# Two more m quarters used unsplit, state reads grouped by pairs, and a wider issue gate in a float32 attention and FFN kernel

## The chip, the cores and the metric

The kernel runs on one core of one Trainium2 chip, in one launch. The metric is the device time of that launch in microseconds; lower is better. "PE" is the matmul engine (TensorE), "PEld" its weight loads, "DVE" the vector engine, "ACT" the scalar engine, "POOL" GpSimd and "SP" the engine that issues the transfers.

## The reference

```python
scores = scale * np.matmul(x, state.transpose(0, 1, 3, 2))   # x: 8 x 8 x 512 x 64, state: 8 x 8 x 32 x 64
scores = scores - scores.max(-1, keepdims=True)
a = np.exp(scores)
a /= a.sum(-1, keepdims=True) + 1e-09
xread = np.matmul(a, state)
scores2 = scale * np.matmul(state, x.transpose(0, 1, 3, 2))
...
sread = np.matmul(a2, x)
attn = np.concatenate([xread, sread], axis=2)
...
h = x @ w_in          # x: 4608 tokens x 512, w_in: 512 x 2048
g = h - np.tanh(h)
return g @ w_out      # w_out: 2048 x 512
```

Everything is float32. `a2` is the softmax of `scores2` over the 512 positions. The 4608 tokens are the 8 x 512 positions read from the state (`xread`) and the 8 x 32 state rows (`sread`).

## The kernel before

**What is multiplied.** `xread` is never formed. For each batch `b` the state is multiplied with `w_in` first: `m` (256 rows of heads and state slots, 2048 columns, held in four quarters `q` of 512 columns), and then `h = a @ m`. The hidden part of a chunk (`Chunk(i)`, one batch `b` of 512 tokens, or the 256 rows of `sread` as the last chunk) has 16 blocks `f` of 128 columns; for each block PE writes one PSUM bank `hps`, ACT takes `tanh` of it into `t`, DVE subtracts (`t = hps - t`), and the output part multiplies `g` with the rows `f` of `w_out` (`wo`) into four banks `ops`, one per 128 tokens, that gather over all `f`.

**Split operands.** A float32 operand is split into two fp32r parts, `hi` and `lo`, by `split`: ACT casts (line 97), DVE subtracts (line 98). A product is then three fp32r matmuls (lines 397 to 399 for the hidden part, 437 to 439 for the output). This holds for `m`, for the attention weights `at` (their split form is `aT`), for `g` and for `wo`. Only quarter 0 of chunk 0 is used unsplit: there `m_first[0]` and the unsplit weights `ats` go into plain float32 matmuls (lines 599 and 395), which the profile shows as two records each.

**The start.** `w_in` and `w_out` come as 64-bit numbers and are made float32 on the chip (`Weight.steps`: three DVE passes, lines 127, 128 and 131, one ACT pass, line 130). The first part is written out by hand as the string `SEQ`; its op `D` is a matmul on a blank tile into a bank that nobody reads, `S` the scores of batch 0, `c`, `T`, `M`, `B`, `E`, `Z`, `N`, `A` the softmax chain of batch 0 up to the transposed weights `ats`. Right behind it `split_first` splits these weights. `m_first_two` multiplies the state of batches 0 and 1 with a row block of `w_in` (line 164) and copies the two halves of the bank to `m_first[q]` and `m_second[q]`.

**The order afterwards.** A list of 144 steps `(chunk, f)`: blocks 0 to 7 of chunk 0, all of chunk 1, blocks 8 to 15 of chunk 0, then chunks 2 to 8. In step `st` the hidden part of step `st + 2` and the output part of step `st` are written. Side work (attention of later batches, conversion of weights, `m` of later batches) is cut into units by `yield`, and tables (`SCH`, `D0`) say at which step each unit is written; `tc.issue_after(x)` keeps what is written inside it behind instruction `x` in the scheduler's order. For steps below `GATED` all side work stands behind the tanh and the subtraction of its step. A scheduler then fixes one order for each engine; each engine runs its queue in that order.

**State reads.** `state_read(b, ss)` is the `sread` part: for each half `hf` (four heads) an exponential of the scores, four PE transposes into `pps`, an ACT copy to `pt`, 16 matmuls of 32 x 64 with the positions `xn` into `rps` (line 351), and four small DVE multiplications into `sr`.

Of the kernel before, what the change touches and what calls it, by code (L numbers as in the profile page):

```python
# [26 lines left out]
EPS = 1e-9  # L27
LAG = 2
HALF = 8
GATED = 48  # L30
EARLY_S = 2
# [4 lines left out]
def attention_ffn(ctx: ExitStack, tc: tile.TileContext, xT, xn, bd, bh, sp, sm, sl, win, wout, xout, sout):  # L36
# [209 lines left out]
    def attention(b, aT):  # L246
# [51 lines left out]
        for hf in range(2):  # L298
            e = es[hf]
            ef = e.rearrange("p a n -> p (a n)")  # L300
            z = pool.tile([P, 16, 1], F32, tag="z", name=f"z{b}{hf}")
            nc.vector.reduce_sum(z, e, axis=AX.X)
            nc.vector.tensor_scalar_add(z, z, EPS)
            nc.vector.reciprocal(z, z)
            nc.vector.tensor_mul(e, e, z.broadcast_to([P, 16, 32]))
            at = pool.tile([P, 512], F32, tag="at", name=f"at{b}{hf}", bufs=1)
            nc.vector.transpose(at, ef)
            yield split(aT[:, 0, hf], aT[:, 1, hf], at)
        if b >= EARLY_S:
# [9 lines left out]
    def split_first():  # L319
        for hf in range(2):  # L320
            split(aTs[0][:, 0, hf], aTs[0][:, 1, hf], ats[hf])

    def state_read(b, ss):
        for hf in range(2):

# [16 lines left out]
            pt = pool.tile([P, 4, P], F32, tag="p2t", name=f"p2t{b}{hf}", bufs=PTB)  # L342
            nc.scalar.copy(pt, ps)
            yield

            w = 1
            ps = bank(ps_a, f"rps{b}{hf}")[:, : 64 * w]
            for k in range(4):
                for c in range(4 // w):
                    cs = slice(32 * w * c, 32 * w * c + 32 * w)  # L350
                    nc.tensor.matmul(  # L351
                        ps[cs], pt[:, k, cs], xr[:, k, 64 * w * c : 64 * w * c + 64 * w], start=(k == 0), stop=(k == 3)
                    )
            for j in range(4):
                h = 4 * hf + j
                js = slice(32 * j, 32 * j + 32)
                nc.vector.tensor_scalar_mul(
                    sr[b // 4][32 * (b % 4) : 32 * (b % 4) + 32, 64 * h : 64 * h + 64],
                    ps[js, 64 * (j % w) : 64 * (j % w) + 64],
                    ri[js],  # L360
                )
            yield

# [11 lines left out]
    class Chunk:  # L375
# [5 lines left out]

        def prepare(self, q):
            self.m[q] = load_m(self.i, q) if self.i < B else load_win(q)

        def hidden(self, f):

            i, n = self.i, self.n
            ps = bank(ps_h, f"hps{i}_{f}")[:, :n]
            cols = slice((f % 4) * P, (f % 4) * P + P)
            mhi, mlo = self.m[f // 4]  # L390
            ahi, alo = aTs[i][:, 0], aTs[i][:, 1]
            nk = 2 if i < B else 4
            for k in range(nk):
                if mlo is None:
                    nc.tensor.matmul(ps, mhi[k][:, cols], ats[k], start=(k == 0), stop=(k == 1))
                    continue
                nc.tensor.matmul(ps, mhi[k][:, cols], ahi[:, k], start=(k == 0), stop=False)  # L397
                nc.tensor.matmul(ps, mhi[k][:, cols], alo[:, k], start=False, stop=False)  # L398
                nc.tensor.matmul(ps, mlo[k][:, cols], ahi[:, k], start=False, stop=(k == nk - 1))  # L399
            self.finish(f, ps)  # L400
# [143 lines left out]
    def step(op):  # L544
# [133 lines left out]
    for st, (i, f) in enumerate(steps):  # L678
# [87 lines left out]
```

## Time and profile before

| | |
|---|---|
| three timed runs | 676.95, 679.95, 681.13 us (median 679.95) |
| the profiled execution | 677.02 us, of which the span of the instructions is 675.2 us |
| PE busy | 653.2 us, 97% of the span |
| DVE busy | 462.1 us, 68% |
| ACT busy | 376.5 us, 56% |
| HBM traffic | 146 GB/s over the span |
| mean granted clock of PE | 0.996 of full speed |

The shares are means over the whole span, and the first tenth of it is unlike the rest: the page's row of forty slices shows DVE at 9 tenths in slices 2, 5 and 6 and PE below that in the first two, and from slice 6 on PE at 9 tenths in every slice to the end, with DVE down to 4 to 7. A matmul's record in the trace is longer than the time until the next one may start, so the starts of neighbouring matmuls are the measure of what one costs.

### The profile page before, as it was taken

What the parts mean: (1) busy time and instruction counts of PE and PEld (TensorE: products, weight loads), DVE (VectorE), ACT (ScalarE), POOL (GpSimd) and SP (SyncE); (2) the same over time, 40 slices, a digit from 0 to 9 for tenths busy, and PEclk for the clock granted to TensorE, in tenths of its full rate; (3) what the DMA queues carried; (4) which work ended last, traced back from release to release, by engine and by line L of the source; (5) the groups of instructions that cost most, each with busy time, mean ns of one, the idle gap of its engine ahead of it and who ended that gap; (6) DMA issues with size and microseconds to landing.
All of it is one profiled execution on the core that took longest, in us unless ns stands there. A gap on an engine that the chain in (4) does not pass through costs nothing.

```text
span 675.2 us, 9423 instructions
## 1 busy us (share of the span) xinstructions
PE 653.2 (97%) x3456; PEld 516.2 (76%) x3456; DVE 462.1 (68%) x811; ACT 376.5 (56%) x667; POOL 1.2 (0%) x7
## 2 busy tenths in 40 slices
PE   5699899999999999999999999999999999999997
PEld 2356677887888877787888787887778788888996
DVE  5989898969766469857975497647664686444442
ACT  3696487867755556855656365535443454333442
POOL 0000000000000000000000000000000000000000
PEclk9899999999999999999999999999999999999999
DMA  8586386566565642825345344553251212000300
GB/s 301 167 289 270 143 274 215 171 186 212 175 193 183 164 167 103 260 83 183 111 164 164 94 128 161 177 168 138 95 172 63 94 63 94 1 29 26 135 31 32
DMA packets 45935, 99.25 MB, mean 147 GB/s; under 512 B 6081, under 2 KB 11457, under 8 KB 45889
## 3 DMA queue, kind: packets, MB, share of 16 engines
q1 hardware_dynamic: 45888, 98.65, 45.0%
q8 instruction: 27, 0.44, 0.3%
q14 instruction: 20, 0.16, 0.1%
HBM read 66.65 MB, written 31.98 MB: 146 GB/s over the span
## 4 chain that ended last, share of the span: by engine, by line
PE 85%; DVE 8%; ACT 2%; DMA 2%; issue 1%; SPq 0%; ACTq 0%; DVEq 0%
PE ops L437 17%; PE ops L439 16%; PE ops L438 16%; PE hps L397 9%; PE hps L398 9%; PE hps L399 9%; PE mps L200 2%; PE rps L351 1%; PE sps L275 1%; PE pps L341 1%; PE mps L164 1%; DMA mr<-md 1%; PE mps L199 1%; DVE m L98 1%; DMA xT<-in_xT 1%
## 5 line engine op out<-in xcount | busy, mean ns | idle before, releaser
L437 PE MATMUL ops<-wo,g 128*128 128x512 f32 x544 | 214.1, 398 | 1.5 <-ACT wo L97 1.5
L438 PE MATMUL ops<-wo,g 128*128 128x512 f32 x544 | 213.0, 392 | 0.0
L439 PE MATMUL ops<-wo,g 128*128 128x512 f32 x544 | 199.2, 391 | 0.3 <-DVE g L98 0.3
L405 DVE TENSOR_TENSOR t<-hps,t 128x512 f32<-128x512 f32 (+1 forms) x142 | 93.5, 658 | 94.5 <-ACT t L405 93.8
L405 ACT ACTIVATE t<-hps 128x512 f32<-128x512 f32 (+1 forms) x142 | 81.3, 573 | 130.1 <-PE hps L399 127.1
L437 PEld LDWEIGHTS ops<-wo,g 128*128 128x128 f32 x544 | 102.6, 189 | 29.8 <-ACT wo L97 3.7
L97 ACT CAST g<-t 128x512 fp32r<-128x512 f32 (+1 forms) x142 | 84.4, 596 | 66.5 <-DVE t L405 63.1
L98 DVE TENSOR_TENSOR g<-t,g 128x512 fp32r<-128x512 f32 (+1 forms) x142 | 93.3, 659 | 41.0 <-ACT g L97 39.3
L439 PEld LDWEIGHTS ops<-wo,g 128*128 128x128 f32 x544 | 102.0, 188 | 23.7 <-issue 1.6
L438 PEld LDWEIGHTS ops<-wo,g 128*128 128x128 f32 x544 | 102.2, 188 | 21.4 <-issue 1.0
L397 PE MATMUL hps<-aT,m 128*128 128x512 f32 x248 | 98.8, 400 | 2.5 <-ACT aT L97 1.4
L398 PE MATMUL hps<-aT,m 128*128 128x512 f32 x248 | 97.1, 392 | 0.2 <-DVE aT L98 0.2
L399 PE MATMUL hps<-aT,m 128*128 128x512 f32 x248 | 96.9, 391 | 0.0
L397 PEld LDWEIGHTS hps<-aT,m 128*128 128x128 f32 x248 | 46.4, 188 | 16.4 <-ACT aT L97 2.7
L399 PEld LDWEIGHTS hps<-aT,m 128*128 128x128 f32 x248 | 46.6, 188 | 11.4 <-DVE wor L127 0.8
L398 PEld LDWEIGHTS hps<-aT,m 128*128 128x128 f32 x248 | 46.6, 188 | 10.7 <-DVE aT L98 1.1
L98 DVE TENSOR_TENSOR wst<-w,wst 64x512 fp32r<-64x512 f32 x64 | 43.9, 686 | 14.7 <-ACT wst L97 12.9
L201 ACT COPY st<-mps 128x512 f32<-128x512 f32 x64 | 36.5, 587 | 18.2 <-PE mps L200 18.1
L98 DVE TENSOR_TENSOR m<-mr,m 128x1024 fp32r<-128x1024 f32 x31 | 37.8, 1220 | 11.2 <-ACT m L97 10.8
L97 ACT CAST wst<-w 64x512 fp32r<-64x512 f32 x64 | 39.6, 619 | 0.8
L97 ACT CAST m<-mr 128x1024 fp32r<-128x1024 f32 x31 | 32.3, 1045 | 7.1 <-DMA mr<-md 7.0
L200 PE MATMUL mps<-wst,sms 128*128 128x512 f32 x64 | 24.9, 395 | 0.0
(216 smaller groups left out, 577.5 us busy)
## 6 DMA issues: line engine op xcount, KB each, us to landing
md<-st SPq DMA_DIRECT2D x128, 128.0 KB, 2.3
mr<-md SPq DMA_DIRECT2D x26, 512.0 KB, 3.8
xT<-in_xT SPq DMA_DIRECT2D x16, 512.0 KB, 4.8
w<-wf SPq DMA_DIRECT2D x16, 512.0 KB, 4.3
xn<-in_xn SPq DMA_DIRECT2D x16, 512.0 KB, 3.4
out_x<-ob SPq DMA_DIRECT2D x32, 256.0 KB, 2.4
wn<-wf SPq DMA_DIRECT2D x8, 512.0 KB, 4.1
ml<-md SPq DMA_DIRECT2D x8, 512.0 KB, 3.8
```

The lines of the kernel that those rows point to most:

```text
L97: nc.scalar.copy(hi, src)
L98: return (sub or nc.vector).tensor_sub(lo, src, hi)
L164: nc.tensor.matmul(ps, sps[:, p], wfs[q, k][:, c], start=True, stop=True)
L200: nc.tensor.matmul(ps, s[:, 0, h], t[:, e], start=(g == 1), stop=True)
L201: nc.scalar.copy(stage[:, e], ps)
L397: nc.tensor.matmul(ps, mhi[k][:, cols], ahi[:, k], start=(k == 0), stop=False)
L398: nc.tensor.matmul(ps, mhi[k][:, cols], alo[:, k], start=False, stop=False)
L399: nc.tensor.matmul(ps, mlo[k][:, cols], ahi[:, k], start=False, stop=(k == nk - 1))
L405: tanhs.append((nc.scalar.activation(t, ps, AF.Tanh).ins, nc.vector.tensor_sub(t, ps, t).ins))
L437: nc.tensor.matmul(o, g[:, 0, tok], wo[:, f, 0], start=first, stop=False)
L438: nc.tensor.matmul(o, g[:, 0, tok], wo[:, f, 1], start=False, stop=False)
L439: return nc.tensor.matmul(o, g[:, 1, tok], wo[:, f, 0], start=False, stop=last).ins
```

## The change

- Quarter 1 of chunk 0 and quarter 0 of chunk 1 are used unsplit, as quarter 0 of chunk 0 was: 8 blocks `f` with two float32 matmuls in place of six fp32r ones, and no split of these two quarters of `m`.
- The weights `aT` of batch 0 are split in steps 9 and 10 in place of right after `SEQ`. Those of batch 1 are kept unsplit in a tile `both` (tag `x`) and split in step 9, as units of their own. `ats` of batch 0 gets buffers of its own.
- Six more `D` at the head of `SEQ`.
- `state_read` does the transposes of both halves first, then the 32 matmuls of both into one bank, then the eight multiplications. Its number of units stays four.
- `GATED` goes from 48 to 144.
- Tables: `a0` [58, 60, 62, 64] becomes [58, 58, 59, 59], `r1` [74, 76, 78, 80] becomes [74, 74, 75, 75], `att0` [2, 3, 4, 5, 5, 6] becomes [2, 3, 4, 5, 5, 9, 9, 10].

```diff
+UNSPLIT = {0: 2, 1: 1}
...
-GATED = 48
+GATED = 144
...
-            at = pool.tile([P, 512], F32, tag="at", name=f"at{b}{hf}", bufs=1)
+            if b == 1:
+                if hf == 0:
+                    both = pool.tile([P, 2, 512], F32, tag="x", name="at1", bufs=XB)
+                at = both[:, hf]
+            else:
+                at = pool.tile([P, 512], F32, tag="at", name=f"at{b}{hf}", bufs=1)
             nc.vector.transpose(at, ef)
-            yield split(aT[:, 0, hf], aT[:, 1, hf], at)
+            if b == 1:
+                ats[1][hf] = at
+            if b != 1:
+                split(aT[:, 0, hf], aT[:, 1, hf], at)
+            yield
+        if b == 1:
+            for hf in range(2):
+                yield split(aT[:, 0, hf], aT[:, 1, hf], both[:, hf])
...
     def split_first():
         for hf in range(2):
-            split(aTs[0][:, 0, hf], aTs[0][:, 1, hf], ats[hf])
+            yield split(aTs[0][:, 0, hf], aTs[0][:, 1, hf], ats[0][hf])
...
             nc.scalar.copy(pt, ps)
+            pts.append(pt)
+            xrs.append(xr)
+            ris.append(ri)
             yield
-            w = 1
-            ps = bank(ps_a, f"rps{b}{hf}")[:, : 64 * w]
+        ps = bank(ps_a, f"rps{b}").rearrange("p (g n) -> p g n", g=2)[:, :, :64]
+        for hf in range(2):
             for k in range(4):
-                for c in range(4 // w):
-                    cs = slice(32 * w * c, 32 * w * c + 32 * w)
+                for c in range(4):
+                    cs = slice(32 * c, 32 * c + 32)
                     nc.tensor.matmul(
-                        ps[cs], pt[:, k, cs], xr[:, k, 64 * w * c : 64 * w * c + 64 * w], start=(k == 0), stop=(k == 3)
+                        ps[cs, hf], pts[hf][:, k, cs], xrs[hf][:, k, 64 * c : 64 * c + 64], start=(k == 0), stop=(k == 3)
                     )
+        yield
...
         def prepare(self, q):
+            if q < UNSPLIT.get(self.i, 0):
+                r = (m_first, m_second)[self.i][q]
+                self.m[q] = [r[:, k] for k in range(2)], None
+                return
...
-                    nc.tensor.matmul(ps, mhi[k][:, cols], ats[k], start=(k == 0), stop=(k == 1))
+                    nc.tensor.matmul(ps, mhi[k][:, cols], ats[i][k], start=(k == 0), stop=(k == 1))
...
             advance(a0, D0["a0"].count(st))
+            if st in [9, 10]:
+                next(first_split)
```

What the scheduler made of it, first on PE, at the output of block 1 of chunk 0 (`ops` from `g_1`), with the product of state and `w_in` for quarter 1 (`mps`) around it. Before:

```order
L437 MATMUL ops_0_3_354<-wo,g_1_266 128x512
L164 MATMUL mps_347<-w_320,sps 128x512
L438 MATMUL ops_0_0_351<-wo,g_1_266 128x512
L439 MATMUL ops_0_0_351<-wo,g_1_266 128x512
L438 MATMUL ops_0_1_352<-wo,g_1_266 128x512
```

And now:

```order
L459 MATMUL ops_0_3_356<-wo,g_1_272 128x512
L417 MATMUL hps_4_422<-at_209,mr_304 128x512
L417 MATMUL hps_5_460<-at_209,mr_304 128x512
L165 MATMUL mps_349<-w_322,sps 128x512
L460 MATMUL ops_0_0_353<-wo,g_1_272 128x512
```

The first float32 halves of blocks 4 and 5 of chunk 0 now stand there; their second halves stand within the output of block 3. Before, all of blocks 4 and 5 stood behind the output of block 3.

On DVE, from the subtraction `t_0` of chunk 1 on (`w` and `wor` are conversions of `w_in` and `w_out`). Before:

```order
L405 TENSOR_TENSOR t_0_624<-hps_0_617,t_0_624 128x512
L127 TENSOR_SCALAR w_679<-w20d 128x512
L127 TENSOR_SCALAR w_679<-w21d 128x512
L127 TENSOR_SCALAR wor_695<-wo8d 128x512
L128 SCALAR_TENSOR_TENSOR w_679<-w20d,w_679 128x512
L128 SCALAR_TENSOR_TENSOR w_679<-w21d,w_679 128x512
L405 TENSOR_TENSOR t_1_649<-hps_1_642,t_1_649 128x512
L127 TENSOR_SCALAR w_734<-w22d 128x512
L128 SCALAR_TENSOR_TENSOR wor_695<-wo8d,wor_695 128x512
L98 TENSOR_TENSOR g_0_627<-t_0_624,g_0_627 128x512
```

And now, from the subtraction `t_1` on:

```order
L427 TENSOR_TENSOR t_1_616<-hps_1_613,t_1_616 128x512
L128 TENSOR_SCALAR w_697<-w22d 128x512
L129 SCALAR_TENSOR_TENSOR wor_662<-wo8d,wor_662 128x512
L99 TENSOR_TENSOR aT_124<-at_209,aT_124 128x512
L132 ISA w_646<-w_646,w20r 128x1024
L99 TENSOR_TENSOR aT_431<-at_562,aT_431 128x512
L132 ISA w_646<-w_646,w21r 128x1024
L99 TENSOR_TENSOR aT_431<-at_562,aT_431 128x512
L99 TENSOR_TENSOR g_0_598<-t_0_595,g_0_598 128x512
```

The rows from `t_0` to `t_1` are as before; between `t_1` and the `lo` part of `g_0` three of the four moved splits and two conversion passes have come in.

On PE, at the state read of batch 2, with the hidden block 2 of chunk 2 around it. Before, the first half (`pps` are the transposes of the second):

```order
L399 MATMUL hps_2_1911<-aT_1283,m_1783 128x512
L397 MATMUL hps_2_1911<-aT_1283,m_1783 128x512
L351 MATMUL rps_1687<-xn_1590,p2t_1597 32x64 x16
L341 MATMUL pps_1719<-ident,s_1401 128x128 x4
L398 MATMUL hps_2_1911<-aT_1283,m_1783 128x512
```

And now, where both halves stand, one block later:

```order
L461 MATMUL ops_0_1_1891<-wo,g_0_1775 128x512
L420 MATMUL hps_3_1906<-aT_1250,m_1762 128x512
L369 MATMUL rps_1672<-xn_1557,p2t_1564 32x64 x16
L369 MATMUL rps_1672<-xn_1663,p2t_1670 32x64 x16
L200 MATMUL mps_1711<-wst_1705,sms_1051 128x512
```

Two stretches of 16 became one of 32. In the whole order there were 16 such stretches, and there are 9: seven of 32 and two of 16.

## Rows read from the trace of the kernel before

**Rows 1.** Windows: stretch, its length; PE, PEld, DVE, ACT, POOL busy us; clock; DMA share; GB/s.
```profile
77.00:115.00 38.00, 37.66 (x150) 28.21 (x151) 35.47 (x64) 29.45 (x52) 0.00 (x0) 1.00 0.67 235
115.00:660.00 545.00, 544.73 (x3012) 441.11 (x3011) 358.61 (x627) 295.94 (x522) 0.00 (x0) 1.00 0.41 131
```

**Rows 2.** Timeline, start and length in us: neighbouring fp32r matmuls, float32 weight loads.
```profile
34.29 0.39 PE L438 MATMUL ops<-wo,g 128*128 128x512 f32 x1
34.52 0.39 PE L439 MATMUL ops<-wo,g 128*128 128x512 f32 x1
...
35.63 0.19 PEld L395 LDWEIGHTS hps<-at,mr 128*128 128x128 f32 x1 [0.24 <-issue]
36.06 0.19 PEld L395 LDWEIGHTS hps<-at,mr 128*128 128x128 f32 x1 [0.24 <-issue]
```

**Rows 3.** Timeline, PE, hidden blocks 0 to 2 of chunk 1.
```profile
72.07 0.73 PE L397 MATMUL hps<-aT,m 128*128 128x512 f32 x2 [1.00 <-ACT aT L97]
...
77.34 0.50 PE L397 MATMUL hps<-aT,m 128*128 128x512 f32 x1 [1.02 <-DVE t L405]
```

**Rows 4.** Timeline of the start, POOL and DVE.
```profile
0.87 0.53 POOL L530 MEMSET blank<- 128x512 f32 x1
...
18.62 0.69 DVE L98 TENSOR_TENSOR aT<-at,aT 128x512 fp32r<-128x512 f32 x1
19.23 0.25 DVE L569 RECIPROCAL z<-z 128x16 f32<-128x16 f32 x1
```

**Rows 5.** Timeline, PE, 39 to 53 us; in brackets idle time before and its end.
```profile
39.77 1.20 PE L437 MATMUL ops<-wo,g 128*128 128x512 f32 x4 [0.98 <-ACT wo L97]
...
45.05 1.19 PE L437 MATMUL ops<-wo,g 128*128 128x512 f32 x4 [0.50 <-ACT wo L97]
...
50.62 0.39 PE L397 MATMUL hps<-aT,m 128*128 128x512 f32 x1
...
52.54 1.06 PE L275 MATMUL sps<-xT,bdr 64*32 64x512 f32 x8 [0.85 <-DMA xT<-in_xT]
```

**Rows 6.** Tile xT: scores matmuls, length in ns (least, median, most).
```profile
L275 PE MATMUL sps<-xT,bdr x112: 587/589/614, 52.5 to 532.5; 64*32 64x512 f32 x112
...
L551 PE MATMUL sps<-xT,bdr x8: 1057/1074/1116, 6.6 to 9.3; 128*64 128x512 f32 x8
```

**Rows 7.** Timeline, DVE, 49 to 80 us.
```profile
49.01 1.22 DVE L98 TENSOR_TENSOR m<-mr,m 128x1024 fp32r<-128x1024 f32 x1
50.14 0.69 DVE L128 SCALAR_TENSOR_TENSOR wor<-wo5d,wor 128x512 uint32<-128x512 uint32 x1
...
71.12 1.25 DVE L460 COPY ob<-ops 128x512 f32<-128x512 f32 x2
72.30 0.67 DVE L98 TENSOR_TENSOR aT<-at,aT 128x512 fp32r<-128x512 f32 x1
73.00 0.71 DVE L307 STREAM_TRANSPOSE at<-e 128x512 f32<-128x512 f32 x1
...
76.59 0.69 DVE L405 TENSOR_TENSOR t<-hps,t 128x512 f32<-128x512 f32 x1 [1.50 <-ACT t L405]
...
79.41 0.69 DVE L405 TENSOR_TENSOR t<-hps,t 128x512 f32<-128x512 f32 x1
```

**Rows 8.** Timeline, PE, around 16 state-read matmuls (32 records) of a half.
```profile
488.56 0.39 PE L398 MATMUL hps<-aT,m 128*128 128x512 f32 x1
488.88 0.65 PE L351 MATMUL rps<-xn,p2t 128*32 128x64 f32 x32
...
489.80 0.40 PE L439 MATMUL ops<-wo,g 128*128 128x512 f32 x1
```

**Rows 9.** Timeline, PE, around the eight scores matmuls (16 records) of batch 2.
```profile
151.99 0.39 PE L438 MATMUL ops<-wo,g 128*128 128x512 f32 x1
152.31 1.09 PE L275 MATMUL sps<-xT,bdr 64*32 64x512 f32 x16
...
153.67 0.39 PE L437 MATMUL ops<-wo,g 128*128 128x512 f32 x1
```

More of the change, by code (lines that the diff above doesn't have):

```diff
@@ L320, in split_first @@
         for hf in range(2):
-            split(aTs[0][:, 0, hf], aTs[0][:, 1, hf], ats[hf])
+            yield split(aTs[0][:, 0, hf], aTs[0][:, 1, hf], ats[0][hf])
     def state_read(b, ss):
+        pts, xrs, ris = [], [], []
         for hf in range(2):
@@ L343, in state_read @@
             nc.scalar.copy(pt, ps)
+            pts.append(pt)
+            xrs.append(xr)
+            ris.append(ri)
             yield
-            w = 1
-            ps = bank(ps_a, f"rps{b}{hf}")[:, : 64 * w]
+        ps = bank(ps_a, f"rps{b}").rearrange("p (g n) -> p g n", g=2)[:, :, :64]
+        for hf in range(2):
             for k in range(4):
-                for c in range(4 // w):
-                    cs = slice(32 * w * c, 32 * w * c + 32 * w)
+                for c in range(4):
+                    cs = slice(32 * c, 32 * c + 32)
                     nc.tensor.matmul(
-                        ps[cs], pt[:, k, cs], xr[:, k, 64 * w * c : 64 * w * c + 64 * w], start=(k == 0), stop=(k == 3)
+                        ps[cs, hf], pts[hf][:, k, cs], xrs[hf][:, k, 64 * c : 64 * c + 64], start=(k == 0), stop=(k == 3)
                     )
+        yield
+        for hf in range(2):
             for j in range(4):
@@ L357, in state_read @@
                 nc.vector.tensor_scalar_mul(
-                    sr[b // 4][32 * (b % 4) : 32 * (b % 4) + 32, 64 * h : 64 * h + 64],
-                    ps[js, 64 * (j % w) : 64 * (j % w) + 64],
-                    ri[js],
+                    sr[b // 4][32 * (b % 4) : 32 * (b % 4) + 32, 64 * h : 64 * h + 64], ps[js, hf], ris[hf][js]
                 )
-            yield
+        yield
     def turn_sread():
@@ L466, in attention_ffn @@
     aTs = [None] * (B + 1)
-    ats = [None] * 2
+    ats = [[None] * 2 for _ in range(2)]
     def new_attention(b):
@@ L572, in step @@
         elif k == "A":
-            ats[j] = pool.tile([P, 512], F32, tag="ob", name=f"at0{j}", bufs=OB)
-            o(nc.vector.transpose(ats[j], es[j]))
+            ats[0][j] = pool.tile([P, 512], F32, tag=f"at0{j}", name=f"at0{j}", bufs=1)
+            o(nc.vector.transpose(ats[0][j], es[j]))
         elif k in "abrp":
@@ L598, in step @@
             i = "hH".index(k)
-            o(nc.tensor.matmul(hps[j], m_first[0][:, i, j * P : j * P + P], ats[i], start=(i == 0), stop=(i == 1)))
+            o(nc.tensor.matmul(hps[j], m_first[0][:, i, j * P : j * P + P], ats[0][i], start=(i == 0), stop=(i == 1)))
         elif k == "X":
@@ L624, in attention_ffn @@
     RE = json.loads('[1, 0, 0, 1]')
-    SEQ = 'a0 r0 b0 p0 S0 c0 T0 S1 D D M0 c1 B0 T1 E0 D D M1 B1 a1 r1 E1 b1 m0 k0 p1 Z0 N0 D A0 m1 k1 Z1 N1 D A1 a2 r2 h0 H0 h1 H1 b2 X0 p2 G0 X1 m2 a3 r3 b3 p3 D m3 k2 D G1 k3'
+    SEQ = 'D D D D D D a0 r0 b0 p0 S0 c0 T0 S1 D D M0 c1 B0 T1 E0 D D M1 B1 a1 r1 E1 b1 m0 k0 p1 Z0 N0 D A0 m1 k1 Z1 N1 D A1 a2 r2 h0 H0 h1 H1 b2 X0 p2 G0 X1 m2 a3 r3 b3 p3 D m3 k2 D G1 k3'
     for op in SEQ.split():
@@ L633, in attention_ffn @@
     a0 = state_read(0, ss)
-    split_first()
+    first_split = split_first()
     late1 = late_read(1)
@@ L647, in attention_ffn @@
     atts = {}
-    SCH = dict(json.loads('{"conv": [0, 1, 8, 8, 9, 10, 11, 12, 13, 14], "pair": [0, 1, 9, 9, 10, 11, 12, 13, 14, 15], "a0": [58, 60, 62, 64], "att0": [2, 3, 4, 5, 5, 6], "att1": [21, 22, 23, 24, 25, 26, 28, 28, 30], "att2": [5, 9, 9, 13, 13, 13, 13, 13, 13], "m0": [17, 18, 19, 20, 21, 22, 23, 24, 25, 26, 27, 28, 30, 31, 33, 35], "m1": [40, 46, 52, 53, 53, 54, 55, 57, 62, 62, 62, 65, 73, 77, 79, 84], "wo": [0, 1, 2, 3, 4, 5, 6, 8, 10, 12, 13, 15, 17, 18, 19], "r1": [74, 76, 78, 80]}'))
+    SCH = dict(json.loads('{"conv": [0, 1, 8, 8, 9, 10, 11, 12, 13, 14], "pair": [0, 1, 9, 9, 10, 11, 12, 13, 14, 15], "a0": [58, 58, 59, 59], "att0": [2, 3, 4, 5, 5, 9, 9, 10], "att1": [21, 22, 23, 24, 25, 26, 28, 28, 30], "att2": [5, 9, 9, 13, 13, 13, 13, 13, 13], "m0": [17, 18, 19, 20, 21, 22, 23, 24, 25, 26, 27, 28, 30, 31, 33, 35], "m1": [40, 46, 52, 53, 53, 54, 55, 57, 62, 62, 62, 65, 73, 77, 79, 84], "wo": [0, 1, 2, 3, 4, 5, 6, 8, 10, 12, 13, 15, 17, 18, 19], "r1": [74, 74, 75, 75]}'))
     D0 = dict(
```

## The prediction

> **What bounds the kernel now.** The page's busy shares come first, PE at 97%, but a record of a PE that waits inside a run counts as busy too, so the share alone cannot say whether there is anything to win. The windows say where: from 115 to 660 us PE is busy for 544.73 of 545 us, with DVE at 359 and ACT at 296 [rows 1]. The starts of neighbouring matmuls show that this is real work: an fp32r matmul of 512 columns starts every 0.23 us (34.29, 34.52), and I use 0.227, which repeats through the steady part [rows 2]. From the last long wait on (77.34 us, block 2 of chunk 1 waiting for the bank of block 0) PE's queue never stands still for half a microsecond [rows 1, 3]. So the time is the moment at which PE becomes continuously fed, now 77 us, plus the PE work left after it. Only two things can help: reach that moment sooner, or take work off PE. Before that moment DVE is the engine behind which the others wait: its queue of conversions and softmax steps runs almost without a gap, and PE waits at 39.77 and 45.05 us for a converted weight, at 72.07 us for the split of the weights of batch 1, and at 77.34 us for a subtraction [rows 3, 5].
>
> **The blank matmuls and the start.** PE stands idle until 6.6 us, so the six blanks cost nothing if they end by then: six times two records of 256 columns. The scores of batch 0 are eight records of 512 columns, issued as four pairs that start between 6.6 and 9.3 us, 0.9 us from pair to pair [rows 6]; half of that is 0.45, and twelve come to 5.4 us from 1.4 us on, when the blank tile is written [rows 4]: 6.8 at that slow pace, sooner at a better one, and the first scores' data is there at 6.6. So between 0 and 0.2 us lost. What they may give: the scores take 1074 ns a record, a like float32 form later 589 ns [rows 6], as if the first ones ran at the lower of the two clock levels (1.2 GHz, not 2.4), although the clock row has no lower entry there. With the upper level, the first scores and so the DVE chain behind them come up to 0.9 us earlier; with the lower one, none. I take 0.5 of the -0.2 to 0.9. *The Trainium skill (TensorE: Matmul & The Clock Gate, Part 1) says that half clock is the default and activity releases it, which would give the full 0.9; no run here shows whether these blanks are enough. By it the sum below would be 0.4 us better.*
>
> **Splits taken out of the DVE chain.** The first split of batch 0's weights stands between two steps of the softmax chain (18.62, next at 19.23): 0.6 us [rows 4]. The second falls where DVE waits for a tanh anyway: 0. So all that follows the start moves by s = 0.6 + 0.5 = 1.1 us (0.5 to 1.5), and ACT, which has no gap of its own work in the stretch behind, passes it on. In the stretch of 49 to 74 us DVE loses two splits of m (1.13 us of queue each: 49.01 to 50.14), the first split of batch 1's weights (0.7: 72.30 to 73.00) and the two copies of finished outputs that stood ahead of the last transpose (1.18: 71.12 to 72.30) [rows 7]: 4.1 us. The last transpose, which ended at 73.7, then ends at 69.6 - s.
>
> **Unsplit blocks on PE.** A float32 record starts 0.43 us after the one before it (35.63, 36.06), a float32 matmul of 512 columns is two of them, 0.86 us [rows 2]. A block costs 2 x 0.86 = 1.72 us in place of 6 x 0.227 = 1.36: PE gets 0.36 more for each of eight blocks. It pays where PE waits anyway. I follow PE's queue in the new order, in the times of before less s:
> - Until the end of block 3's output (50.62 us before [rows 5]) the float32 halves of blocks 4 and 5 come in, 4 x 0.86 = 3.44. They fill the wait of 0.50 at 45.05 and some 0.15 more: 53.4.
> - Then the scores of batch 1 in one run instead of two, 1.2 us (its price is worked out below; their input lands at about 52.5 [rows 5], which is in time), blocks 6 and 7 (3.44) and 48 output matmuls (10.9): 69.0. Before, PE came to this place at 71 and waited.
> - Blocks 0 and 1 of chunk 1 need no split: their first halves need the first transpose, their second halves (70.7) the last one (69.6). PE does not wait; it ends at 72.4. Block 2 needs the bank of block 0: tanh and subtraction after 71.6. Before, the subtraction began at 76.59 and block 2 at 77.34 [rows 7, 3]; with a tanh of 0.6 it starts at 73.2 where it was 77.34. That is 4.1 us, and s on top.
> - Given back: blocks 2 and 3 cost 0.36 more each (0.7). Block 3 needs the bank of block 1, and five conversion passes are queued on DVE ahead of that subtraction, which came 2.8 us behind the first (76.59, 79.41 [rows 7]): from 72.6 on it ends at 76.1. PE, which now comes at 74.9, waits some 1.1 us.
>
> Front: 4.1 + 1.1 - 0.7 - 1.1 = 3.4 us won.
>
> **The moved splits.** All four of the weights' splits now come to DVE right after that, at 0.6 us each, 2.4 us, in a stretch where DVE is busy for 35.47 of 38 us [rows 1]. What hides them: DVE starts this stretch 4 us earlier too, and PE waited for nothing in it. Behind the three that stand ahead of `g_0`'s low part waits only the last third of block 0's output, which PE's queue reaches two float32 matmuls and eight output matmuls later. I take 0; if the cover is gone, up to the whole front gain.
>
> **State reads in one group.** A run of 16 state-read matmuls takes PE from 488.56 to 489.80 us, 1.24 us, of which two ordinary matmuls are 0.45: 0.79 us. The 32 records themselves follow each other at 14 ns (0.45); the other 0.34 us is the change to another shape and back [rows 8]. Seven runs fewer save 7 x 0.34 = 2.4 us; I take 2.0, since before some runs shared that change with transposes next to them. *The Trainium skill (TensorEngine Tiling (Array Packing), Key Properties) says that changing the tiling mode drains the engine, which the row agrees with. (TensorE: Matmul & The Clock Gate, Part 3, the mechanism) adds only about 4 ns for each further tile; the row shows 14 ns a record. By the page's price a group of 32 would cost 0.3 us less and the sum would be 2.3 us better; the row's price stands in the sum.* The scores of one later batch stand in one run less: a run costs 153.67 - 151.99 - 0.45 = 1.2 us [rows 9], nearly all of it the same change of shape. Together 3.2 us less PE work after the front.
>
> **The gate.** In the stretch that it adds, PE has 0.27 us of idle time in 545 [rows 1]; there is nothing to win. It could cost, if weights of a next batch came late: from 0 up to the rival below. I take 0.
>
> **Sum.** 3.4 + 1.2 + 2.0 = 6.6 us. The profiled execution of before took 677.02 us (675.2 us of span), which gives 670.4; against the median of the three runs, 679.95, it is 673.4, and I give that, as medians are what will be compared. The runs of before lie 4 us apart, so a change below 1% (6.8 us) can hardly be told from none.
>
> **The rivals.**
> 1. *The front gain is given back.* PE becomes fed 3.4 us sooner, but DVE has no less to do before 115 us apart from two m splits (2.3 us), and if a conversion (weights of block 8, m of quarter 2) is the next thing late, PE waits there. For it: DVE at 93% in that window [rows 1]. Against it: not one wait of PE there before. Then 3.2 us stay: 676.7.
> 2. *More than the sum.* The blanks give 0.9, DVE is less loaded than I count and the 1.1 us at block 3 does not come: 6.6 + 0.4 + 1.1 = 8.1: 671.9.
> 3. *Slower: the grouped state read stops PE's queue.* The queue is strict, and all that follows a group waits with it. Before, the first half's matmuls needed one copy and one load; a group needs both. In the new order the group stands some 20 ordinary matmuls, 4.5 us, behind the second half's transposes. If exponential, transposes, copy and load of `xn` take longer than that on queues that now carry side work behind every tanh, each of eight reads stops PE for the rest. It decides from 0.8 us a read on (8 x 0.8 = 6.6); for over 1% slower it takes 1.7. With 2.5 us: 8 x 2.5 - 6.6 = +13.4, 693. Against it: the same copies and loads were never waited for in 545 us.
> 4. *The change does not do what it says.* Had the scheduler left its order as it was, the time would stay at 679.95; the order shows the moves, so this has no chance of its own.
>
> **How the numbers follow.** The forecast (gains of 4 to 7.5 us) 0.54, rival 1 0.20, rival 2 0.20, rival 3 0.06. Faster by over 1% needs more than 6.8 us: all of rival 2 and a third of the forecast, 0.38. Slower by over 1% is rival 3, 0.06. Within 1%: 0.56. The range takes in rival 1 (676.7) and rival 2 (671.9), with 2 us on each side for the spread of the runs: 670 to 678.5.
>
> **What would show it.** Right: float32 records of blocks 4 and 5 between 38 and 52 us, block 2 of chunk 1 starting near 72 us, four splits on DVE near 76 to 82 us, PE idle in 115 to 660 us still under 1 us, 32-matmul state reads of about 1.24 us. Wrong: PE waiting between 75 and 110 us for a DVE conversion (rival 1), or before state reads (rival 3); scores of batch 0 still at 1074 ns a record (no clock gain).

## The result and the profile after

| | median | runs | ratio to before, 95% interval |
|---|---|---|---|
| before, beside the first runs | 679.87 us | 676.95 to 681.13, 6 | |
| changed kernel | 670.11 us | 668.49 to 671.66, 6 | 0.9879 [0.9855, 0.9902] |
| changed kernel once more, other chip | 669.56 us | 667.80 to 670.31, 6 | 0.9859 [0.9830, 0.9888] |

Faster, by 1.2 to 1.4%, 8 to 10 us by the ratios. The profiled execution of the changed kernel took 671.66 us, that of before 677.02: only 5.4 us apart. Why two profiles lie 5.4 us apart and two medians 9.8 is half of what the experiments were for.

Windows of the changed kernel (stretch, its length; PE, PEld, DVE, ACT, POOL busy; clock; DMA share; GB/s), against [rows 1]:
```profile
77.00:115.00 38.00, 37.68 (x147) 27.61 (x148) 35.90 (x64) 29.59 (x52) 0.00 (x0) 1.00 0.74 249
115.00:660.00 545.00, 545.00 (x3044) 445.94 (x3043) 358.76 (x630) 297.23 (x525) 0.00 (x0) 1.00 0.41 131
```
PE still has no idle time behind 115 us, and the time is still "when PE becomes continuously fed, plus the work left". So I read each run by two numbers: the start of block 2 of chunk 1 (77.34 us before [rows 3]), and the rest, the span minus it. Before: 675.2 - 77.3 = 597.9 us.

Timeline, PE, hidden blocks 0 to 3 of chunk 1 in the changed kernel's first profile:
```profile
70.30 3.59 PE L417 MATMUL hps<-at,mr 128*128 128x512 f32 x8
74.51 1.98 PE L417 MATMUL hps<-at,mr 128*128 128x512 f32 x4 [0.61 <-DVE t L427]
77.32 1.13 PE L417 MATMUL hps<-at,mr 128*128 128x512 f32 x2 [0.83 <-DVE t L427]
```
The same in its second profile (run f1_after_again):
```profile
68.14 3.59 PE L417 MATMUL hps<-at,mr 128*128 128x512 f32 x8
72.35 1.98 PE L417 MATMUL hps<-at,mr 128*128 128x512 f32 x4 [0.61 <-DVE t L427]
75.16 1.12 PE L417 MATMUL hps<-at,mr 128*128 128x512 f32 x2 [0.83 <-DVE t L427]
```
Equal patterns, 2.2 us apart; the rest is 595.4 in both. Most of what moved the first one is in the windows of these two executions around 40 us:
```profile
40.31:43.72 3.41, 3.41 (x5) 1.51 (x5) 3.41 (x8) 2.67 (x5) 0.00 (x0) 0.50 1.00 306
```
```profile
40.00:43.40 3.40, 3.40 (x10) 1.83 (x11) 3.40 (x8) 2.95 (x5) 0.00 (x0) 1.00 0.86 276
```
In the first profile the granted clock was at the lower level (0.50, 1.2 GHz) from 40.3 to 43.7 us, and PE got half as many records done; in the second at the upper one (2.4 GHz). Timeline, PE, the matmuls ahead of and behind that stretch, in the first profile and then in the second:
```profile
39.34 1.28 PE L459 MATMUL ops<-wo,g 128*128 128x512 f32 x4 [2.03 <-ACT wo L98]
...
43.91 1.02 PE L165 MATMUL mps<-w,sps 128*128 128x512 f32 x2
```
```profile
38.75 1.19 PE L459 MATMUL ops<-wo,g 128*128 128x512 f32 x4 [0.98 <-ACT wo L98]
...
41.75 1.02 PE L165 MATMUL mps<-w,sps 128*128 128x512 f32 x2
```
The first profile ran 0.6 us late ahead of the fall (39.34, 38.75) and 2.2 late after it (43.91, 41.75), so this fall cost 1.6 us. The 0.6 was there before; the first profile had another fall at 19.8 us, the second one at 27.5.

Tile xT, the scores of batch 0 (length in ns: least, median, most), in the changed kernel and then without its six blanks (run e1_no_blanks); before it was 1074 [rows 6]:
```profile
L573 PE MATMUL sps<-xT,bdr x8: 592/618/643, 6.6 to 8.6; 128*64 128x512 f32 x8
```
```profile
L573 PE MATMUL sps<-xT,bdr x8: 1061/1061/1114, 6.5 to 9.2; 128*64 128x512 f32 x8
```
Timeline, DVE, of the changed kernel's first profile, against [rows 7]: the last transposes right ahead of the copies, and the four splits of attention weights behind the two subtractions (the first and the last are shown):
```profile
69.27 1.30 DVE L314 STREAM_TRANSPOSE at<-e 128x512 f32<-128x512 f32 x2
70.49 1.25 DVE L482 COPY ob<-ops 128x512 f32<-128x512 f32 x2
73.76 0.69 DVE L427 TENSOR_TENSOR t<-hps,t 128x512 f32<-128x512 f32 x1 [2.02 <-ACT t L427]
...
76.60 0.67 DVE L427 TENSOR_TENSOR t<-hps,t 128x512 f32<-128x512 f32 x1
...
78.13 0.67 DVE L99 TENSOR_TENSOR aT<-at,aT 128x512 fp32r<-128x512 f32 x1
...
83.28 0.67 DVE L99 TENSOR_TENSOR aT<-at,aT 128x512 fp32r<-128x512 f32 x1
```
Timeline, PE, a grouped state read, against [rows 8]:
```profile
481.98 0.39 PE L421 MATMUL hps<-aT,m 128*128 128x512 f32 x1
482.30 1.10 PE L369 MATMUL rps<-xn,p2t 128*32 128x64 f32 x64
483.33 0.50 PE L419 MATMUL hps<-aT,m 128*128 128x512 f32 x1
483.67 0.40 PE L420 MATMUL hps<-aT,m 128*128 128x512 f32 x1
```
From 481.98 to 483.67, less two ordinary matmuls (0.45): 1.23 us for 64 records, against 0.79 for 32. So 32 more records cost 0.45, 14 ns each, and the change of shape is 0.34 us, as worked out. The Trainium skill (TensorE: Matmul & The Clock Gate, Part 3, the mechanism) has some 4 ns for a further tile of a pack. Here only four column strips take turns, each many times, and a record adds 14 ns, so the page's price is not one for these groups.

### The profile page after: what moved, and what is told of

Same layout as the page of the kernel before. It is cut to its first block, busy times and chain, and to the rows that moved or that the text cites. A ratio compares the mean times of both kernels' runs of the same rounds, so it can differ in the third digit from the quotient of the medians.

```text
span 669.9 us, 9418 instructions
## 1 busy us (share of the span) xinstructions
PE 654.2 (98%) x3452; PEld 517.9 (77%) x3452; DVE 458.7 (68%) x809; ACT 375.0 (56%) x665; POOL 1.2 (0%) x7
## 3 DMA queue, kind: packets, MB, share of 16 engines
q1 hardware_dynamic: 45888, 98.65, 45.4%
## 4 chain that ended last, share of the span: by engine, by line
PE 95%; DVE 2%; ACT 1%; DMA 1%; issue 0%; POOL 0%; ACTq 0%; DVEq 0%; POOLq 0%
PE ops L459 19%; PE ops L460 18%; PE ops L461 18%; PE hps L419 9%; PE hps L420 9%; PE hps L421 9%; PE mps L201 2%; PE hps L417 2%; PE sps L276 1%; PE mps L165 1%; PE rps L369 1%; PE mps L200 1%; PE pps L356 1%; DMA wo2d<-in_wout 1%; PE warm L569 1%; PE hps L621 1%
## 5 line engine op out<-in xcount | busy, mean ns | idle before, releaser
L419 PE MATMUL hps<-aT,m 128*128 128x512 f32 x232 | 91.6, 395 | 0.0
L420 PE MATMUL hps<-aT,m 128*128 128x512 f32 x232 | 90.8, 391 | 0.0
L421 PE MATMUL hps<-aT,m 128*128 128x512 f32 x232 | 90.4, 389 | 0.0
L419 PEld LDWEIGHTS hps<-aT,m 128*128 128x128 f32 x232 | 43.6, 188 | 9.5 <-DVE g L99 0.2
L420 PEld LDWEIGHTS hps<-aT,m 128*128 128x128 f32 x232 | 43.6, 188 | 9.4 <-issue 0.5
L421 PEld LDWEIGHTS hps<-aT,m 128*128 128x128 f32 x232 | 43.6, 188 | 9.1
L202 ACT COPY st<-mps 128x512 f32<-128x512 f32 x64 | 36.6, 588 | 18.3 <-PE mps L201 18.0
L99 DVE TENSOR_TENSOR m<-mr,m 128x1024 fp32r<-128x1024 f32 x29 | 35.4, 1222 | 11.7 <-ACT m L98 8.5
L98 ACT CAST m<-mr 128x1024 fp32r<-128x1024 f32 x29 | 30.3, 1045 | 6.8 <-DMA mr<-md 6.7
L201 PE MATMUL mps<-wst,sms 128*128 128x512 f32 x64 | 24.5, 393 | 0.0
```

Of the source, the lines that this page charges most:

```text
L98: nc.scalar.copy(hi, src)
L99: return (sub or nc.vector).tensor_sub(lo, src, hi)
L201: nc.tensor.matmul(ps, s[:, 0, h], t[:, e], start=(g == 1), stop=True)
L202: nc.scalar.copy(stage[:, e], ps)
```

## The experiments

Start and rest (us) from the profiles; the stretches at the lower clock ahead of 100 us stand beside them, since they decide the start:

| run | edit | start of block 2 | rest | lower clock (us) | median | ratio, interval |
|---|---|---|---|---|---|---|
| before | | 77.34 | 597.9 | 28.6-32.0 | 679.87 | |
| g3_before_again | none | 80.12 | 597.4 | 16.1-19.5, 40.0-46.8 | 679.29 (one) | |
| g1_before_more_blanks | 24 blanks | 77.74 | 597.7 | 40.4-43.8 | 676.45 | 0.9974 [0.9954, 0.9993] |
| g4_before_group | grouping alone | 79.71 | 594.8 | 16.5-26.7, 30.1-33.5 | 676.34 | 0.9983 [0.9963, 1.0004] |
| changed kernel | | 74.51 | 595.4 | 19.8-23.2, 40.3-43.7 | 670.11 | 0.9879 [0.9855, 0.9902] |
| f1_after_again | none | 72.35 | 595.4 | 27.5-30.9 | 669.56 | 0.9859 [0.9830, 0.9888] |
| e1_no_blanks | without 6 blanks | 72.08 | 595.3 | none | 670.24 | 0.9893 [0.9871, 0.9915] |
| e2_old_reads | without grouping | 72.90 | 598.7 | 27.5-30.9 | 674.72 | 0.9948 [0.9928, 0.9968] |
| e3_split_again | without unsplit quarters | 78.60 | 593.5 | 14.7-18.1, 28.3-31.7, 42.0-45.4 | 673.85 | 0.9939 [0.9913, 0.9965] |
| e4_gate48 | gate as before | 71.05 | 595.8 | 15.5-18.9 | 669.94 | 0.9891 [0.9868, 0.9913] |
| f2_more_blanks | 18 more blanks | 71.35 | 597.4 | none | 670.63 | 0.9875 [0.9846, 0.9904] |
| g2_more_blanks_again | the same | 71.46 | 599.1 | none | 669.98 | 0.9885 [0.9856, 0.9914] |
| f3_un12 | one quarter more unsplit | 70.89 | 596.7 | 14.9-18.3 | 671.06 | 0.9884 [0.9851, 0.9916] |
| f4_gate48_out4 | gate as before, 4 output buffers | 74.35 | 595.0 | 20.2-23.6, 40.7-44.1 | 669.61 | 0.9856 [0.9821, 0.9890] |

**e1_no_blanks**
```diff
-    SEQ = 'D D D D D D a0 r0 b0 p0 S0
+    SEQ = 'a0 r0 b0 p0 S0
```


> The changed kernel without its six blank matmuls. By the sum of the prediction the blanks bring the start forward by 0.5 to 0.9 us through the upper clock level at the first scores, so this run should be 0.5 to 0.9 us slower than the changed kernel (670.6 to 671.0), with the first scores back at about 1074 ns a record. Rival: the blanks also decide when the clock falls in the first 45 us (in the profile of the changed kernel it fell at 19.8 and 40.3 us, in that of the kernel before once, at 28.6 us), and each fall costs up to 1.7 us on PE; then this run differs by more than 1.5 us from the changed kernel, either way, and the clock row of its profile shows the fall at another place.

The scores are back at 1061 ns, as expected, and the second halves of blocks 0 and 1 start at 20.45 us where f1 has 19.95. The time is not told apart from the changed kernel's (intervals overlap widely). The start shows why: 72.08 with no fall of the clock at all, against 71.05 and 70.89 (e4, f3) with blanks and a fall only at 15 us, where PE mostly waits, and 72.35 with a fall at 27.5. So by these single profiles the blanks are worth 1.0 to 1.2 us, a little above the bound (0.9), and one fall of the clock takes it back. The Trainium skill (TensorE: Matmul & The Clock Gate, Part 1) says that activity releases the half clock; the lengths of the records agree, 618 ns with six blanks and 1061 without, though the clock row shows no lower entry there.

**e2_old_reads**
```diff
-        ps = bank(ps_a, f"rps{b}").rearrange("p (g n) -> p g n", g=2)[:, :, :64]
-        for hf in range(2):
+            ps = bank(ps_a, f"rps{b}{hf}")[:, : 64 * w]
...
-"a0": [58, 58, 59, 59]
+"a0": [58, 60, 62, 64]
```


> The changed kernel with the state reads of each half in a run of 16 matmuls again, and their four steps at the old places. By the sum of the prediction each of seven to eight further runs costs 0.34 us: 2.0 to 2.7 us; the order has one scores run less than the changed kernel, 1.2 us back. So 0.8 to 1.5 us slower than the changed kernel: 670.9 to 671.6. Rival: the grouping is worth what the time shows beyond the sum (about 3 us more than the 2.0 taken); then this run is 3 us or more slower than the changed kernel, 673 or above.

4.7 us slower by the ratios, and 674.72 lies where the rival had it (673 or above). The rest is 3.4 us longer than the changed kernel's. But the small runs (matmuls of smaller shapes, each run priced as in [rows 8, 9]) behind 100 us take only 0.7 us more, near the 0.8 to 1.5 of the first theory; most of the others are two new waits, of 1.4 and 0.9 us. Timeline, PE and DVE, at the first:
```profile
343.97 0.50 PE L415 MATMUL hps<-aT,m 128*128 128x512 f32 x1 [1.11 <-DVE t L423]
```
```profile
342.62 0.69 DVE L478 COPY ob<-ops 128x512 f32<-128x512 f32 x1 [1.31 <-DMA out_x<-ob]
343.23 0.68 DVE L423 TENSOR_TENSOR t<-hps,t 128x512 f32<-128x512 f32 x1
```
A copy of a finished output waits on DVE for its buffer's store, the subtraction behind tanh stands after it, and PE waits for the bank. That is a property of this order, not the price of the runs; the rival (grouping worth 3 us more for itself) is not borne out.

**e3_split_again**
```diff
-UNSPLIT = {0: 2, 1: 1}
+UNSPLIT = {}
...
-"att0": [2, 3, 4, 5, 5, 9, 9, 10]
+"att0": [2, 3, 4, 5, 5, 6]
```


> The changed kernel with quarter 1 of chunk 0 and quarter 0 of chunk 1 split into two fp32r parts again, and the splits of both attention weights at their old places; blanks, grouping and gate stay. By the prediction this takes back 4.1 + 0.6 - 0.7 - 1.1 = 2.9 us, and the order has one scores run more, 1.2 us: 4.1 us slower than the changed kernel, about 674.2, with block 2 of chunk 1 starting near 77 us instead of 74.5. Rival 1 of the prediction (the gain at the front is given back to DVE later): at most 1.2 us slower than the changed kernel. Rival that the unsplit quarters are worth more than their term: 6 us or more slower.

4.1 us slower by the ratios (0.9939 to 0.9879), 673.85: both numbers of the first expectation. Its start is 78.60 where 77 was said, with three falls of the clock ahead of it. The rest tells it without the clock: 593.5, so the unsplit quarters cost 1.8 us behind block 2's start, where the prediction had 0.7 + 1.1. Compared with before, this kernel has all but the unsplit quarters and the moved splits, and its rest is 4.1 us shorter (597.6, the mean of three profiles, less 593.5).

**e4_gate48**
```diff
-GATED = 144
+GATED = 48
```


> The changed kernel with the side work held back behind tanh only up to step 48, as before. By the prediction the gate is worth 0: the order has two scores runs less and four stretches of small shapes more (33 in place of 29), so -2.4 us for the first and up to 1.4 us for the second: 669 to 670. Rival: the gate itself is worth something that the sum left out; then this run is slower than the changed kernel by 1.5 us or more.

The same time as the changed kernel. The small runs behind 100 us sum to 24.5 us instead of 27.1, and the rest is still 0.4 longer: 2.6 us went into two waits. Timeline, PE, then ACT, then DVE:
```profile
265.99 0.39 PE L201 MATMUL mps<-wst,sms 128*128 128x512 f32 x1
267.01 0.50 PE L201 MATMUL mps<-wst,sms 128*128 128x512 f32 x1 [0.63 <-ACT st L202]
269.08 0.50 PE L419 MATMUL hps<-aT,m 128*128 128x512 f32 x1 [1.57 <-DVE t L427]
```
```profile
265.09 1.26 ACT L98 CAST wst<-w 64x512 fp32r<-64x512 f32 x2
266.37 0.58 ACT L202 COPY st<-mps 128x512 f32<-128x512 f32 x1
```
```profile
265.74 1.41 DVE L99 TENSOR_TENSOR wst<-w,wst 64x512 fp32r<-64x512 f32 x2 [0.34 <-ACT wst L98]
267.61 0.69 DVE L482 COPY ob<-ops 128x512 f32<-128x512 f32 x1 [0.47 <-DMA out_x<-ob]
268.33 1.29 DVE L427 TENSOR_TENSOR t<-hps,t 128x512 f32<-128x512 f32 x2
```
Side work stands ahead of what PE needs on two engines: on ACT two casts of weights (`wst`) ahead of the copy `st` that ends PE's first wait, on DVE two splits of `wst` and an output copy ahead of the subtraction that ends the second. Under the wide gate, in the changed kernel's first profile, neither engine has `wst` work between 266 and 274 us. So the gate does something, but in this kernel it wins 2.6 us of waits and pays as much in further changes of shape.

**f1_after_again** (the changed kernel, no edit)

> The changed kernel once more, on the chip of the runs beside it. By the sum of the prediction it is 6.6 us faster than the kernel before at equal clocks (ratio 0.990); the first runs gave 0.988, 8.2 us. If the rest is only the luck of how often the clock fell in the start of either kernel, then runs with the same mean clock differ by 6 to 7 us, and the ratio lies between 0.988 and 0.991. Rival: a term is mis-sized for good; then runs of equal clock differ by 8 us or more.

The rival's value by the ratio (9.6 us); by the profiles it lies between the two: 667.7 against 675.2 us of span, both with one fall of the clock at 28 us, is 7.5. The mean clock of each run tells more. Before, over the 55 runs beside these experiments: 30 runs with a mean clock of 0.996 or more took 676.8 us in the mean, 22 runs at 0.994 or less 680.5. The changed kernel, both measurements: 669.3 (7 runs) and 670.5 (4 runs). At a high clock they are 7.4 us apart (7.2 on this run's chip alone, 4 and 3 runs), again between the two expectations; the medians add what the falls cost the kernel before.

**f2_more_blanks** (18 more blanks; the text on record counts one too many)
```diff
-E1 b1 m0 k0
+E1 b1 D D D D D D m0 k0
...
-N1 D A1 a2 r2 h0 H0
+N1 D D D D A1 a2 r2 h0 D D D D H0
...
-b3 p3 D m3
+b3 p3 D D D D D D m3
```


> The changed kernel with 19 more blank matmuls in four places of the start at which PE waits (ahead of m0, ahead of and behind the first half of block 0, ahead of m3). Theory: PE's stillness there is what goes before the falls of the clock to its lower level, each of which costs 1.0 to 1.3 us (slope of time over mean clock in the runs so far); with the gaps filled the clock falls less often: mean clock 0.998 or more in most runs, 1 to 2 us faster than the changed kernel, and less spread. Rival: the falls come from something else; then clocks stay at 0.994 to 0.997 and the time is the same or up to 1 us longer where blanks hold up real work.

The clock half came true, the time half not. Mean clock 0.999 to 1.0 in all six runs, and the start of block 2 at 71.35. But in the profile PE stood still for 1.9 us at 487 us. Timeline, PE, of this run and of f1, then the loads of the inputs on SP's queue:
```profile
486.86 0.39 PE L421 MATMUL hps<-aT,m 128*128 128x512 f32 x1
489.18 1.05 PE L276 MATMUL sps<-xT,bdr 64*32 64x512 f32 x4 [1.93 <-issue]
```
```profile
487.87 0.39 PE L421 MATMUL hps<-aT,m 128*128 128x512 f32 x1
488.19 1.05 PE L276 MATMUL sps<-xT,bdr 64*32 64x512 f32 x4
```
```profile
480.64 1.77 SPq L260 DMA_DIRECT2D xT<-in_xT  x2
```
```profile
481.69 1.65 SPq L260 DMA_DIRECT2D xT<-in_xT  x2
```
Issued as long ahead of the scores as in f1, the loads of batch 7's inputs took 8.4 us to land instead of 5.7 (medians of the two loads): 480.64 and 8.4 is 489.0, just ahead of the matmul that waited. g2 below met the same wait.

**f3_un12**
```diff
-UNSPLIT = {0: 2, 1: 1}
+UNSPLIT = {0: 2, 1: 2}
```


> The changed kernel with one more quarter unsplit, quarter 1 of chunk 1 (blocks 4 to 7, behind the last wait of PE). By the prediction float32 blocks cost PE 0.36 us each more and pay only where PE waits: four blocks, 1.4 us slower than the changed kernel, and no gain, since PE waits for nothing from there on. Rival: DVE, which loses a split of 1.2 us in a stretch where it is busy for 95 of 100, gives something back: same or faster.

1.5 us slower by the medians, with intervals that overlap; the rest is 596.7 against 595.4, 1.3 us for four blocks, 0.34 each where 0.36 was worked out. DVE's freed time gave nothing back. A float32 block costs PE a third of a microsecond more where PE does not wait.

**f4_gate48_out4**
```diff
-GATED = 144
+GATED = 48
...
+            if i >= 2 and t > 1:
+                tag, bufs = "cr", CB
```


> The gate at step 48 as before, and from chunk 2 on finished outputs leave through four buffers in place of two. In the run with the gate alone PE stood still for 2.6 us at 266 to 269 us: a subtraction behind tanh stood on DVE behind a copy of a finished output that waited for its buffer's store, and the small-shape runs cost 2.5 us less than in the changed kernel. If that reading is right, the buffers take the 2.6 us away: 2.5 us faster than the changed kernel, 667.5. Rival: the subtraction would have waited for the copies themselves (0.7 us each); then 0 to 1 us faster only.

Not 2.5 us: the same time as e4 and the changed kernel, and 0.8 us off the rest. Timeline, PE, at the place of e4's waits:
```profile
270.31 0.49 PE L201 MATMUL mps<-wst,sms 128*128 128x512 f32 x1 [0.69 <-ACT st L202]
271.53 0.50 PE L419 MATMUL hps<-aT,m 128*128 128x512 f32 x1 [0.73 <-DVE t L427]
```
DVE, then ACT, at the same place:
```profile
269.04 1.40 DVE L99 TENSOR_TENSOR wst<-w,wst 64x512 fp32r<-64x512 f32 x2
270.79 1.29 DVE L427 TENSOR_TENSOR t<-hps,t 128x512 f32<-128x512 f32 x2 [0.34 <-ACT t L427]
```
```profile
268.38 1.27 ACT L98 CAST wst<-w 64x512 fp32r<-64x512 f32 x2
269.67 0.59 ACT L202 COPY st<-mps 128x512 f32<-128x512 f32 x1
270.15 1.09 ACT L427 ACTIVATE t<-hps 128x512 f32<-128x512 f32 x2
```
The wait for the store is gone, and 1.8 of the 2.6 us stayed. The size is the rival's, its reason (the output copies themselves) is not: `st` and the tanh stood on ACT behind two casts of `wst`, and the subtraction on DVE, its splits done, waited another 0.34 us for that tanh. My reading of e4 explained 0.8 of its 2.6 us; the rest stands mainly on ACT, which it did not look at.

**g1_before_more_blanks** (the blanks of f2 and the six at the start, in the kernel before)
```diff
-    SEQ = 'a0 r0 b0 p0 S0
+    SEQ = 'D D D D D D a0 r0 b0 p0 S0
...
-E1 b1 m0 k0
+E1 b1 D D D D D D m0 k0
...
-N1 D A1 a2 r2 h0 H0
+N1 D D D D A1 a2 r2 h0 D D D D H0
...
-b3 p3 D m3
+b3 p3 D D D D D D m3
```

> The kernel before with the six blanks at its start and the 18 further ones in the waits of PE (24 in all), nothing else changed. Theory: the kernel before loses some 2 to 3 us in the median to falls of the clock in its first 60 us (its runs with a mean clock of 0.997 or more take 675.5 to 677.8 us, those at 0.992 or less 679 to 682). With the clock held up it runs at 675 to 676.5 in all runs with little spread, ratio 0.995 to 0.997. Then the difference to the changed kernel with the same blanks is the prediction's sum without the clock, 6.1 us or near it. Rival: the falls are a symptom and cost nothing by themselves; then its median stays at 678 to 680.

As the theory had it: mean clock 0.997 to 1.0 in 12 runs, 675.2 to 677.8 us with none above, where 23 runs of before beside them reached 681.0; mean 676.3 against 678.0, ratio 0.997. A fall at 40 us still came in the profiled run. So the blanks saved the kernel before 1.6 us in the mean here. They compute nothing, so I put this down to the clock.

**g2_more_blanks_again** (f2 without a further edit)

> The changed kernel with 18 further blanks once more, beside the kernel before with the same blanks. Theory: clock 1.0 in all runs, and 5.5 to 6.6 us faster than the kernel before with blanks: 669 to 670.5. In its first profile one load of batch 7's inputs took 8.4 us to land and PE waited 1.9 us for it; if that was chance, the time is 668.5 to 669.5 here, if it belongs to the kernel 670.5 again.

6.2 us (means 670.1 and 676.3) below the kernel before with the same blanks. The long load was there again (wait 2.3 us, and the clock fell at its end, 489.4 to 492.8 us); if every run had the wait, the difference without it would be near 8 (an estimate, 6.2 + 1.9). Two of two profiles with the further blanks show it, and none of the other eight of the changed kernel and its variants. Why the load is slower there stays open; it is why these blanks did not pay.

**g3_before_again** (the kernel before, no edit)

> The kernel before once more, for a second profile. If the clock falls two or three times in it (as in about half of its runs), the profile should show falls at places where PE bounds the work (30 to 60 us), and a time of 679 to 682; with none or one fall 675.5 to 678.

A run with two falls: 679.29 us, as expected for it. Window of its second low clock, and on PE an output ahead of it, which began at 39.77 in the first profile [rows 5], and block 0 of chunk 1, which began at 72.07 [rows 3]:
```profile
39.98:46.80 6.82, 6.40 (x12) 3.98 (x13) 6.15 (x11) 5.24 (x10) 0.00 (x0) 0.50 0.78 263
```
```profile
40.02 2.08 PE L437 MATMUL ops<-wo,g 128*128 128x512 f32 x4 [2.51 <-ACT wo L97]
...
74.86 0.73 PE L397 MATMUL hps<-aT,m 128*128 128x512 f32 x2 [1.00 <-ACT aT L97]
```
0.25 us later ahead of the fall, 2.8 after it, and all that follows with it; the rest is the same to 0.5. The other low stretch, at 16 us, lies where PE waits for DVE anyway.

**g4_before_group**
```diff
-            ps = bank(ps_a, f"rps{b}{hf}")[:, : 64 * w]
+        ps = bank(ps_a, f"rps{b}").rearrange("p (g n) -> p g n", g=2)[:, :, :64]
...
-"r1": [74, 76, 78, 80]
+"r1": [74, 74, 75, 75]
```


> The kernel before with the state reads in one group of 32 matmuls, and nothing else of the change. By the prediction seven runs less save 2.0 to 2.4 us of PE, and the order has one scores run less, 1.2 us: 3.2 to 3.6 us faster than before, ratio 0.995. Rival: with the gate left at step 48 the grouping brings a wait near 265 us, as in the run of the changed kernel with the old gate (2.6 us there); then 0.5 to 1 us faster only, ratio 0.999.

By time alone it is the rival's (0 to 0.4% faster; 0.995 lies outside the interval). The trace shows both: the rest is 2.8 us shorter than before (mean of three profiles), and PE waits where e4's PE waited. Timeline, PE:
```profile
265.26 0.73 PE L443 MATMUL ops<-wo,g 128*128 128x512 f32 x2 [0.62 <-DVE g L98]
...
274.69 0.50 PE L200 MATMUL mps<-wst,sms 128*128 128x512 f32 x1 [0.63 <-ACT st L201]
...
276.74 0.50 PE L401 MATMUL hps<-aT,m 128*128 128x512 f32 x1 [1.56 <-DVE t L409]
```
These starts are 3.4 us late in all. The grouping brings such waits with the old gate in both kernels.

No run beats the changed kernel by more than its uncertainty.

## Why the prediction was right and wrong

The time lies inside the range by 0.1 us (670.1; 670.0 to 678.5), which is luck: the 2 us below rival 2 were given for the spread of the runs. The case called likeliest, within 1%, did not come: it is 1.2% faster. The mechanisms were right nearly everywhere; the step that failed is the base to which the sum was applied.

- **Front, 3.4 us.** Block 2 was to start 5.2 us sooner (4.1 + s of 1.1); from the profile of before to f1, both with one fall at 28 us, it is 5.0. Given back: 0.7 for float32 (0.34 a block in f3, 0.36 worked out) and 0.83 of wait at block 3 where 1.1 was said; e3 shows both together as 1.8. Right in sum; but the blanks gave 0.5 more than s held, so, if the fall at 28 us cost both kernels the same, the other terms gave some 0.7 less than their 4.7. Which of them is not shown.
- **Blanks.** Taken at 0.5 of a possible 0.9; they give 1.0 to 1.2 where no fall follows at 20 to 43 us, and nothing that a median shows (e1).
- **Moved splits, 0.** Right: they stand at 78 to 84 us, and PE waits for nothing there.
- **State reads and scores, 3.2 us.** The small runs behind 100 us, each priced as in [rows 8, 9], sum to 30.1 us before and 27.1 after: 3.0. The rest shrank by 4.1 (e3). In the first profile of before some 0.6 of the other 1.1 are two waits near 262 and 272 us that the sum took for nothing (0.2 in its two other profiles); what remains was not traced.
- **Gate, 0.** The net is zero (e4), for a reason that the prediction did not see: grouped reads under the old gate leave side work and output copies on ACT and DVE ahead of results that PE waits for, 2.6 us in e4 and 3.4 in g4. "PE has 0.27 us of idle time" was read from the kernel before; under the old gate the grouped order has more, and that is what the gate takes away. Rival 3 looked for such a wait at the reads themselves; it came from the side work.
- **Rival 1** (front given back) is excluded by the rest of e3 and f1: nothing but the 1.8 us. **Rival 2** (671.9) named gains that partly came, but not the one that counts.
- **Sum and base.** 6.6 us was said; at equal clocks it is 7.5 (profiles) or 7.4 (30 and 7 runs). The step "against the median of the three runs, 679.95, it is 673.4" added the 2.9 us between profile and median to both kernels. As far as g1 and g3 show, they are time at the lower clock: the median of before held it, its profile, with no fall near 40 us, did not, and the changed kernel's runs held less (1.2 us between its high and low runs, 3.8 before). How much of it a median of before holds changes from set to set: 679.87, 678.59, 679.47 and 677.15 us beside the four sets of runs. Set against the profiled 677.02 the same sum gives 670.4, and 670.1 was measured, a closeness that is partly luck: the gain is 0.8 to 0.9 larger than the sum, and the median of the changed kernel holds some low clock too. Whether low clocks are rarer in the changed kernel is not shown: 4 of its 12 runs had a mean of 0.994 or less, 22 of 55 before; that they cost it less rests on those 4 runs. In the two pairs of profiles the fall at 40 us itself delays it by 1.6 us and the kernel before by 2.5 (0.25 late ahead of it, 2.8 late at block 2: 80.12, 77.34), in a stretch twice as long.

## What to carry to other kernels

Split the span at the last place where the bounding engine waits, and compare start and rest apart: here the rest repeated to 0.1 us in three profiles of the changed order (to 0.5 in three of before, which has small waits left), where medians of six runs could not tell 1.5 us. Before a sum is set against a median, look at what the mean clock of each run says of the spread, since low-clock time that lies ahead of that place is part of the base and need not carry over. An edit that costs nothing on the engine it names (a gate, a grouping) still reorders the queues of other engines; what stands ahead of a result that the bounding engine needs is the thing to look at.

## What the runs showed of the hardware

- The granted clock fell to half for some stretch ahead of 50 us in 11 of the 14 profiles, behind places where PE had waited 1.3 to 2.5 us, and in g2 at 489.4 us, at the end of a wait of 2.3 us. Such waits also passed without a fall (e1, 1.9 us until 27.1; f2, 1.9 us until 489.2). Where it falls decides the price: none visible at 15 us (70.89 and 71.05 are the earliest starts of all), 1.3 us at 27.5 (72.35 against 71.0), 1.6 us at 40.3 (2.2 late after it, 0.6 late ahead of it).
- With blank matmuls in those waits it fell less (mean clock 0.999 to 1.0 in six runs, 0.997 to 1.0 in six and twelve others), not never: g1's profile has a fall at 40.4 us.
- A change of tile shape costs PE the same for 32 and for 64 small records: 0.34 us, of which one part stands ahead of the run (0.32 us from the last ordinary matmul instead of 0.23) and one behind it, where the second ordinary matmul again starts 0.34 us after the first; the remainder lies between the last small record and the first ordinary matmul (64 records at 14 ns are 0.90 of the 1.03 us from 482.30 to 483.33).
- The same 2 x 512 KB of loads, issued at the same distance, landed in 5.7 us in one kernel (f1) and 8.4 us in another (f2) that differs from it only in blank matmuls, the last of them some 450 us earlier.
